# A K/V attention kernel whose V loads are issued from two queues: some of them from ScalarE's, beside transposing K waves on SyncE's

## The chip, the cores and the metric

The kernel runs on one core of one Trainium2 chip. The metric is the device time of a launch in microseconds (us); lower is better. A core has TensorE (matrix multiply, PE in the profile), VectorE (DVE), ScalarE (ACT), GpSimd (POOL) and SyncE (SP), which here issues DMA transfers and nothing else. Each engine runs its own list of instructions in order, and the lists meet in semaphores. All transfers of a core are carried by its 16 DMA engines.

## What is computed

Two attention blocks, A and B, of the same shapes and with inputs of their own. For each of them, with batch 16, 144 query rows, width 448, 16 heads of 256, and 512 cached keys:

```python
q = (x @ wq).reshape(B, Sq, H, Dh).transpose(0, 2, 1, 3)
scores = einsum("bhqd,bhkd->bhqk", q, k_cache) * (Dh ** -0.5)
p = softmax(scores, axis=-1)
o = einsum("bhqk,bhkd->bhqd", p, v_cache)
out = o.transpose(0, 2, 1, 3).reshape(B, Sq, H * Dh) @ wo
```

The results of A and B lie side by side in the last axis of the output. All is bf16. K and V of one (batch, head) pair are 256 KB each; all 512 pairs are read once, K and V, 268 MB in all.

## The kernel before

**Units and steps.** The work is cut into NT = 512 units, one (block, batch, head) each: 0 to 255 are block A ("pass A"), 256 to 511 block B ("pass B"). A main loop over steps `i` writes every engine's list. In step `i` TensorE gets, in this order, the query projection of a unit some steps ahead (`t_q`; mostly for two batches at once), the scores of unit `i` + 3 (`t_s`, line 1112; two steps ahead for the first 48 units), the value product of unit `i` (`t_pv`, line 1168), for every second unit a matmul with ones that adds up the softmax's denominators (line 1184), and a few matmuls of the output projection (line 1284). ScalarE turns scores into exponentials (line 1122, two instructions a unit), and takes logarithm and exponential of the denominators (lines 1192 and 1205), so as to divide. VectorE moves results out of PSUM; GpSimd adds exponentials up. A step takes TensorE some 2 us.

**K.** The scores need K with its head dimension on the partitions. The first 48 units (P0) have K loaded plainly and transposed on TensorE (`t_load_n`, `t_tr`). All later units get theirs by a transposing DMA, in 29 "waves" of 16 units (`t_load_k`, line 988; 4.19 MB each). `kt_sb` holds 32 units (KR), two waves: a wave may be issued once the wave two before it has been used up, so when the scores of its last unit are done.

**V.** A V load (`t_load_v`, line 1002) brings two units (UV), 512 KB. `v_sb` has nine slots (NV), used in turn in the order in which V loads (and the plain K loads of the start) are planned; `ring_free` keeps the step after which each of them is used up, and `v_seq` the place of each load in this order. The slot's semaphore `v0` to `v8` tells TensorE that it has landed.

**Other loads.** `wq` (query weights of a block, in groups of heads), `wo` (output weights, eight groups of 448 KB), and `x` (transposing too, a few batches at a time) are loaded for both blocks; for B as their places come free, which is around the change of pass, near unit 256. Stores of 112 KB go out 36 times.

**Order of the loads.** All DMA is issued from SyncE's queue, in one order that a planner makes at build time. It has a model of TensorE's time (`clock`, read by `at(i)`: when step `i` begins), for each load a due time (`at` of the step of first use, less MARGIN), the step from which its place is free, and a price in us: 1.44 for a V load, 2.0 + 0.97 a unit for a K wave, 1.3 for a wo group, 0.65 a head for wq. It then fills `dma_plan` one by one, keeping `now`, the time at which the DMA engines would be done with what is planned so far, and `slip`, the most that a load has been late. Of the loads that could start first it takes the one that is due first, save that a K wave yields to a load that would be due before the wave were done, and is taken ahead of loads that can wait for it:

```python
elif k_new:
    better = best[1] > start + m[2] + HOLD
```

The main loop then puts each planned load into SyncE's list in the step from which its place is free. SyncE takes them strictly in that order: a load whose place is still in use holds up all that follow.

**Dependencies.** `S.add(engine, ...)` (class `_Sched`) puts an instruction at the end of an engine's list, with waits for all that wrote or read its buffers before, as far as this engine has not waited for it already. So an instruction added to ScalarE's list at the start of step `i` stands ahead of the exponentials of that step, and what it waits for holds up ScalarE.

Of the kernel before, what the change touches and what calls it, by code (L numbers as in the profile page):

```python
# [12 lines left out]
PE, ACT, DVE, POOL, SP = "pe", "act", "dve", "pool", "sp"  # L13
# [110 lines left out]
def _general_path(  # L124
# [48 lines left out]
    NSG = NT // 8  # L173
    NXGT = NP * Bn // XB

# [410 lines left out]
    s_min = -LQ - 24  # L586
    for XG in range(NXGT):
        pr, j = divmod(XG, Bn // XB)
# [164 lines left out]
def bass_concat_heads__mha_block_cached__gqa_block_cached__near_ridge_kernel(  # L753
# [28 lines left out]
    NT = NP * NU  # L782
    UV = 2
# [11 lines left out]
    NV, NX = 9, 6  # L795
# [8 lines left out]
    RC = RS * 128  # L804
    OP_DELAY, OP_START, OP_RATE = 2, (28, 16), (1.04, 1.15)
    MARGIN, HOLD = 1.0, 1.0
    NXGT = len(X_GROUPS)

    P0 = NNAT * UV
# [11 lines left out]
    with contextlib.ExitStack() as es:  # L821
# [35 lines left out]
        S = _Sched()  # L857
# [31 lines left out]
        def of_step(lead, i):  # L889
            return [u for u in (i + lead(0), i + lead(NT)) if 0 <= u < NT and u - lead(u) == i]  # L890
# [100 lines left out]
        def v_source(t, G):  # L991
            pr, b, h0 = unit(UV * G)
            if unit(UV * G + 1)[1] != b:
                return t[pr][b:b + UV, h0].rearrange("u (p c) d -> p u (c d)", p=128)
            return t[pr][b, h0:h0 + UV].rearrange("u (p c) d -> p u (c d)", p=128)

        def t_load_v(G):
            sl = v_seq["v", G] % NV
            src = v_source(vs, G)

            def e(q):
                return q.dma_start(v_sb[:, sl, :, :], src).then_inc(sems["v%d" % sl], 16)  # L1002
            S.add(SP, e, writes=[(("v", sl), ("v", G))], dma_sem="v%d" % sl, name="v%d" % G)

        def t_load_n(G, j=None):
            sl = v_seq["n", G] % NV
# [37 lines left out]
        def q_pair(U):  # L1044

            b, h = unit(U)[1:]
            if U < P0 or h % 2 and b in (0, Bn - 1):
                return 1
            if b % 2 == h % 2:
                return 2  # L1050
            return 0 if U - H >= P0 else 1
# [217 lines left out]
        def chunk_rows(r):  # L1269
            pr, rl = divmod(r, NCH)  # L1270
            row0 = rl * 128
            m = min(128, Bn * SQ - row0)
            return pr, row0, m
# [34 lines left out]
        def t_store(r):  # L1308
            pr, row0, m = chunk_rows(r)
            sl = r % NOST  # L1310

            def e(q):
                return q.dma_start(of[row0:row0 + m, pr * D:(pr + 1) * D], ost_sb[0:m, sl, :]).then_inc(
                    sems["ost%d" % sl], 16)
            S.add(SP, e, reads=[(("ost", sl), r)], dma_sem="ost%d" % sl, name="st%d" % r)
# [62 lines left out]
        def at(i):  # L1378
            return clock[max(i, s_min)]
# [14 lines left out]
        def load_list():  # L1394
            made = []

            def load(use, free, took, fn, *args):
                made.append((at(use) - MARGIN, free, took, fn, args))

            for XG, (g0, g1) in enumerate(X_GROUPS):  # L1400
                load(first_q[g0], (g1 - NX) * H - lq(NT) if g1 > NX else s_min, 1.3 + 0.55 * (g1 - g0), t_load_x, XG)
            for W, (u0, u1) in enumerate(WAVES):
                last = u1 - 1 - KR
                load(u0 - ls(u0), last - ls(last) + 1 if last >= 0 else s_min, 2.0 + 0.97 * (u1 - u0), t_load_k, W)
            for pr in range(NP):
                for h0, h1 in WQ_GROUPS if pr == 0 else [(h, h + 4) for h in range(0, H, 4)]:
                    load(first_h[pr, h0], NU - H + h1 - lq(NU) if pr else s_min, 0.65 * (h1 - h0), t_load_wq, pr, h0, h1)
                for wg in range(NWG):
                    load(wo_use[pr, wg], wo_done[pr - 1, wg] + 1 if pr else s_min, 1.3, t_load_wo, pr, wg)
            for u in range(4):  # L1410
                load(u - LT, s_min, 0.72, t_load_n, u // 2, u % 2)
            for G in range(2, NNAT):
                load(UV * G - LT, None, 1.44, t_load_n, G)
            for G in range(NT // UV):
                load(UV * G, None, 1.44, t_load_v, G)
            return made

        todo = sorted(load_list(), key=lambda m: m[0])
        dma_plan, due, ring_free, now, slip = [], [], [], 2.0, 0.0
        first = [(t_load_n, (0, 0)), (t_load_x, (0,)), (t_load_wq, (0, 0, 1)), (t_load_n, (0, 1))]  # L1420
        v_seq = {("n", 0): 0, ("n", 1): 1}
        ring_free.extend([UV - LT, 2 * UV - LT])
        while todo:
            n = len(ring_free)
            v_lo = ring_free[n - NV] if n >= NV else s_min
            best = None
            for m in todo[:60]:
                lo = v_lo if m[1] is None else m[1]
                start = max(now, at(lo) + slip if lo > s_min else now)
                latest = m[0] + slip - m[2]  # L1430
                if len(first) and m[3:] == first[0]:
                    best = (start, -1e9, m, lo)
                    break
                if best is None or max(start, now) < max(best[0], now):
                    best = (start, latest, m, lo)
                elif max(start, now) == max(best[0], now):
                    k_new, k_old = m[3] is t_load_k, best[2][3] is t_load_k
                    if k_new == k_old:
                        better = latest < best[1]
                    elif k_new:  # L1440
                        better = best[1] > start + m[2] + HOLD
                    else:
                        better = latest <= start + best[2][2] + HOLD
                    if better:
                        best = (start, latest, m, lo)
            if first:
                first.pop(0)
            now, _latest, m, lo = best
            now += m[2] - (1.0 if m[3] is t_load_k and dma_plan and dma_plan[-1][0] is t_load_k else 0.0)
            slip = max(slip, now - m[0])  # L1450
            todo.remove(m)
            dma_plan.append(m[3:])
            due.append(lo)
            if m[1] is None:
                v_seq["n" if m[3] is t_load_n else "v", m[4][0]] = len(ring_free)
                ring_free.append(UV * (m[4][0] + 1) - (LT if m[3] is t_load_n else 0))

        stores = []
        flag_ev = None
        i = s_min  # L1460
        while i < NT or i in op_at or dma_plan or stores:
            while dma_plan and due[0] <= i:
                fn, args = dma_plan.pop(0)
                due.pop(0)
                if fn is t_load_v:
                    while stores and stores[0][1] <= i:
                        t_store(stores.pop(0)[0])
                fn(*args)
            while stores and (stores[0][1] <= i - STORE_LAG or not dma_plan and stores[0][1] <= i):
                t_store(stores.pop(0)[0])  # L1470
            u = i + LT
            if 0 <= u < P0:
                t_tr(u, 0)
            for u in of_step(lq, i):
                if q_pair(u):
                    t_q(u)
                    t_evac_q(u)
            for u in of_step(ls, i):
                t_s(u)
            u = i + LT  # L1480
            if 0 <= u < P0:
                t_tr(u, 1)
            u = i
            if P0 <= u < NT and u % 2:
                t_recip(u)
            if 0 <= u < NT:
                t_pv(u)
                if u < P0 or u % 2 == 0:
                    t_sum(u)
            if u == P0 - 1:  # L1490
                t_pair_ones()
            if P0 <= u + 2 < NT:
                t_halves(u + 2)
            for u in of_step(ls, i):
                t_presum(u)
            u = i
            if 0 <= u < NT:
                if u < P0 or u % 2 == 0:
                    t_ln(u)
                    t_recip(u)  # L1500
                    t_check(u)
                t_evac_ot(u)
                if u == NT - 1:
                    flag_ev = t_flag()
            for bank, r, cs in op_at.get(i, ()):
                t_op_piece(r, cs, bank)
                if cs[-1] == op_last:
                    t_evac_op(r, bank, ACT if bank == "op" else DVE)
                    stores.append((r, i + (2 if i < NT else 0)))
            i += 1  # L1510
# [80 lines left out]
```

## Time and profile before

The time is 1054.97 us (median of three runs, 1054.96 to 1055.44); the profiled execution has a span of 1051.6 us.

| what | before |
|---|---|
| TensorE busy, share of the span | 1029.9 us, 98% |
| ScalarE busy | 794.1 us, 76% |
| VectorE busy | 737.7 us, 70% |
| GpSimd busy | 636.2 us, 61% |
| mean DMA rate | 280 GB/s |
| K waves: count, median from issue to landing | 29, 21.8 us (B) and 21.7 us (A) |
| V loads: count, median from issue to landing | 256, 7.0 us (B) and 6.9 us (A) |

Busy time counts arithmetic alone; issuing a DMA is not counted as busy for the engine that does it, and is shown as the work of its sequencer (SPq for SyncE, ACTq for ScalarE). In a line of the timeline the columns are start and length in us, engine, line of the kernel, operation, output<-input, number of instructions, and in brackets the idle time before it with what ended it. In the table of stretches each row gives a stretch, its length, the busy time of each engine with its number of instructions, and then the granted clock of TensorE, the DMA engines' share (it can be over 1, where packets overlap) and GB/s. The list of waits has total, times and longest, in us.

### The profile page before, as it was taken

The numbers are of one execution on the slowest core, as the hardware profiler recorded it, in microseconds if no ns is written. First come the engines' busy times: TensorE is split into PE (matmuls) and PEld (weight loads), VectorE is DVE, ScalarE is ACT, GpSimd is POOL, SyncE is SP. The second block draws the span as 40 slices with busy tenths as digits, with TensorE's granted clock in tenths as the row PEclk, the third lists the DMA queues.
The fourth block names the chain that finished last, engine by engine and source line by source line (L and its number), as shares of the span: only waits on it lengthen the run. The fifth ranks groups of instructions, "written<-read, shape, count | busy, mean of one in ns | idle before, by whom it ended". The sixth has DMA issues, their size and how long they took to land.

```text
span 1051.6 us, 32329 instructions
## 1 busy us (share of the span) xinstructions
PE 1029.9 (98%) x12376; PEld 875.8 (83%) x12376; DVE 737.7 (70%) x2039; ACT 794.1 (76%) x2365; POOL 636.2 (61%) x1030
## 2 busy tenths in 40 slices
PE   7999999999999999999999799999999999999998
PEld 6999888888888888888888688888888888888885
DVE  5776676777776776676777567677776667777775
ACT  5877677777777787777877567787877777788785
POOL 3555556666666666666756456566666666666673
PEclk9999999999999999999999999999999999999999
DMA  9999999999999999999999999999999999999950
GB/s 291 363 341 340 263 306 266 288 288 293 290 300 284 285 237 257 302 290 297 265 288 340 268 276 300 295 272 300 282 269 269 299 258 305 302 271 257 289 187 14
DMA packets 591748, 294.14 MB, mean 280 GB/s; under 512 B 502592, under 2 KB 516768, under 8 KB 591584
## 3 DMA queue, kind: packets, MB, share of 16 engines
q1 hardware_dynamic: 591584, 291.99, 110.1%
q8 instruction: 99, 1.62, 0.6%
q14 instruction: 65, 0.53, 0.2%
HBM read 161.48 MB, written 4.13 MB: 157 GB/s over the span
## 4 chain that ended last, share of the span: by engine, by line
PE 90%; DMA 6%; SPq 1%; ACT 1%; DVE 1%; issue 0%; POOL 0%; ACTq 0%; DVEq 0%
PE s_ps L1112 23%; PE ot_ps L1168 23%; PE qp_ps L1081 22%; PE op_ps L1284 19%; DMA kt_sb<-in_B_k_cache_dram 2%; DMA kt_sb<-in_A_k_cache_dram 2%; PE ot_ps L1184 2%; DMA wq_sb<-in_A_wq_dram 1%; PE qp_ps L1032 1%; PE s_ps L1032 1%; PE qp_ps L1284 1%; ACT rinv_sb L1205 1%; DMA v_sb<-in_B_v_cache_dram 0%; SPq L1002 0%; ACT pt_sb L1122 0%
## 5 line engine op out<-in xcount | busy, mean ns | idle before, releaser
L1132 POOL TENSOR_TENSOR pp_sb<-pt_sb 128x288 f32<-128x288 bf16 x512 | 384.6, 751 | 320.1 <-ACT pt_sb L1122 305.4
L1122 ACT ACTIVATE pt_sb<-s_ps 128x288 bf16<-128x288 f32 x1024 | 364.6, 408 | 182.7 <-PE s_ps L1112 176.5
L1220 DVE TENSOR_TENSOR ring<-ot_ps,rinv_sb 128x288 bf16<-128x288 f32 (+2 forms) x640 | 241.8, 394 | 159.4 <-ACT rinv_sb L1205 155.0
L1112 PE MATMUL s_ps<-qt_sb,kt_sb 128*128 128x144 bf16 x4096 | 341.3, 227 | 8.0 <-DMA kt_sb<-in_B_k_cache_dram 6.9
L1168 PE MATMUL ot_ps<-pt_sb,v_sb 128*128 128x144 bf16 x4096 | 340.2, 226 | 0.3 <-DMA v_sb<-in_A_v_cache_dram 0.2
L1112 PEld LDWEIGHTS s_ps<-qt_sb,kt_sb 128*128 128x128 bf16 x4096 | 288.3, 98 | 60.0 <-issue 7.3
L1205 ACT ACTIVATE rinv_sb<-ln_sb 64x144 f32<-64x144 f32 x928 | 298.3, 321 | 24.2
L1081 PE MATMUL qp_ps<-xt_sb,wq_sb 128*128 128x288 bf16 (+1 forms) x2368 | 302.3, 271 | 2.2 <-DMA wq_sb<-in_A_wq_dram 1.2
L1284 PE MATMUL op_ps<-wo_sb,ring 128*128 128x448 bf16 x1120 | 285.5, 352 | 0.0
L1081 PEld LDWEIGHTS qp_ps<-xt_sb,wq_sb 128*128 128x128 bf16 x2368 | 212.7, 98 | 77.1 <-DVE qt_sb L1094 2.3
L1168 PEld LDWEIGHTS ot_ps<-pt_sb,v_sb 128*128 128x128 bf16 x4096 | 274.3, 98 | 1.2 <-DMA v_sb<-in_A_v_cache_dram 0.4
L1137 POOL TENSOR_TENSOR p_sb<-pp_sb 128x144 f32<-128x144 f32 x464 | 227.4, 490 | 74.2 <-DVE ps_sb L1146 9.4
L1235 DVE TENSOR_REDUCE run_sb<-ot_ps 128x1 bf16<-128x144 f32 x560 | 146.5, 304 | 76.7 <-ACT ln_sb L1192 42.6
L1146 DVE TENSOR_TENSOR ps_sb<-p_sb 64x144 bf16<-64x144 f32 x464 | 156.1, 336 | 45.8 <-POOL p_sb L1137 32.5
L1095 DVE CAST qt_sb<-qp_ps 128x576 bf16<-128x576 f32 x216 | 162.1, 750 | 14.0 <-PE qp_ps L1081 10.9
L1284 PEld LDWEIGHTS op_ps<-wo_sb,ring 128*128 128x128 bf16 x1120 | 93.7, 98 | 20.1
L1192 ACT ACTIVATE ln_sb<-ot_ps 128x144 f32<-128x144 f32 x232 | 67.9, 293 | 32.3 <-PE ot_ps L1184 24.5
L1184 PE MATMUL ot_ps<-ps_sb,ones 128*128 128x144 bf16 x280 | 63.3, 226 | 0.0
L1094 DVE CAST qt_sb<-qp_ps 128x288 bf16<-128x288 f32 x80 | 35.8, 447 | 2.8 <-PE qp_ps L1081 2.6
L1040 ACT ACTIVATE kt_sb<-qp_ps 128x512 bf16<-128x512 bf16 x48 | 28.9, 603 | 6.1 <-PE qp_ps L1032 6.1
L1137 POOL TENSOR_TENSOR ps_sb<-pp_sb 128x144 bf16<-128x144 f32 x48 | 23.5, 490 | 6.9 <-PE ot_ps L1184 0.3
L1184 PEld LDWEIGHTS ot_ps<-ps_sb,ones 128*128 128x128 bf16 x280 | 27.4, 98 | 0.0
(29 smaller groups left out, 154.5 us busy)
## 6 DMA issues: line engine op xcount, KB each, us to landing
v_sb<-in_A_v_cache_dram SPq DMA_DIRECT2D x128, 512.0 KB, 6.9
v_sb<-in_B_v_cache_dram SPq DMA_DIRECT2D x128, 512.0 KB, 7.0
v_sb<-in_A_k_cache_dram SPq DMA_DIRECT2D x22, 512.0 KB, 9.9
out_dram<-ost_sb SPq DMA_DIRECT2D x36, 112.0 KB, 6.1
wo_sb<-in_A_wo_dram SPq DMA_DIRECT2D x8, 448.0 KB, 8.5
wo_sb<-in_B_wo_dram SPq DMA_DIRECT2D x8, 448.0 KB, 8.7
wq_sb<-in_B_wq_dram SPq DMA_DIRECT2D x4, 768.0 KB, 9.3
wq_sb<-in_A_wq_dram SPq DMA_DIRECT2D x3, 768.0 KB, 9.2
```

What stands on the lines that cost most here:

```text
L1081: ins = t.matmul(acc, lhsT=wq_sb[:, kc, c0:c0 + 128], rhs=xt_sb[:, kc, xo:xe + 1:max(xe - xo, 1), :], start=(kc == 0), stop=(kc == 3))
L1095: return v.tensor_copy(qt_sb[:, a:b + 1:b - a, :, :], qp_ps[:, :, 0:2 * SQ].rearrange("p e (u q) -> p u e q", u=2))
L1112: ins = t.matmul(s_ps[bank][:, (c % 2) * SQ:(c % 2 + 1) * SQ], lhsT=kt_sb[:, 2 * c + dc, ko:ko + 128], rhs=qt_sb[:, qsl, dc, :], start=(dc ...
L1122: return a.activation(pt_sb[:, psl, 2 * k:2 * k + 2, :].rearrange("p b q -> p (b q)"), s_ps[bank][:, 0:2 * SQ], AF.Exp, scale=DH ** -0.5)
L1132: return g.tensor_tensor(pp_sb[:, :, :], pt_sb[:, psl, 0:2, :], pt_sb[:, psl, 2:4, :], op=ALU.add)
L1137: return g.tensor_tensor(dst, pp_sb[:, 0, :], pp_sb[:, 1, :], op=ALU.add)
L1146: return v.tensor_tensor(ps_sb[p0:p0 + 64, sl, :], p2_sb[0:64, :], p2_sb[64:128, :], op=ALU.add)
L1168: ins = t.matmul(ot_ps[ob][:, dc * SQ:(dc + 1) * SQ], lhsT=v_sb[:, vsl, j, c * DH + dc * 128:c * DH + (dc + 1) * 128], rhs=pt_sb[:, sl, c, ...
L1205: return a.activation(rinv_sb[p0:p0 + 64, sl, :], ln_sb[h0:h0 + 64, :], AF.Exp, scale=-1.0)
L1220: ins = v.tensor_tensor(ring[:, 2 * h:2 * h + 2, r0:r0 + q1 - q0], ot_ps[ob][:, 0:2 * SQ].rearrange("p (c q) -> p c q", c=2)[:, :, q0:q1], ...
L1235: return v.tensor_reduce(run_sb[:, k, j:j + 1], ot_ps[ob][:, 2 * SQ:3 * SQ], axis=AX.X, op=op)
L1284: ins = t.matmul(acc[0:m, 0:D], lhsT=ring[:, c, col0:col0 + m], rhs=wo_sb[:, c, :], start=(c == op_first), stop=(c == op_last))
```

## The change

After the planner has placed a K wave that is planned with more than 15 us, it takes up to three of the next V loads out of its list. Each is meant for a moment 3, 7 and 11 us after the wave's start by the model (WITH_K): it is put into the first step at or after that moment in which its slot is free, if that step begins at least 2 us ahead of the end of the wave by the model and the load is due within 40 us of the step; otherwise no more are taken for this wave. `now` grows by 0.9 us for each, where a V load in SyncE's order costs 1.44. At the start of that step the main loop adds the load to ScalarE's list, ahead of the step's exponentials. Slots, semaphores and sources are the same; a V load planned so takes its place in the turn of the slots like any other. The purpose is that V loads need not stand in SyncE's queue behind a wave, and that two queues have packets for the DMA engines while the wave runs.

```diff
--- before.py
+++ after.py
@@ -804,6 +804,7 @@
     RC = RS * 128
     OP_DELAY, OP_START, OP_RATE = 2, (28, 16), (1.04, 1.15)
     MARGIN, HOLD = 1.0, 1.0
+    WITH_K = (3.0, 7.0, 11.0)
     NXGT = len(X_GROUPS)
 
     P0 = NNAT * UV
@@ -994,13 +995,14 @@
                 return t[pr][b:b + UV, h0].rearrange("u (p c) d -> p u (c d)", p=128)
             return t[pr][b, h0:h0 + UV].rearrange("u (p c) d -> p u (c d)", p=128)
 
-        def t_load_v(G):
+        def t_load_v(G, queue=SP):
             sl = v_seq["v", G] % NV
             src = v_source(vs, G)
 
             def e(q):
                 return q.dma_start(v_sb[:, sl, :, :], src).then_inc(sems["v%d" % sl], 16)
-            S.add(SP, e, writes=[(("v", sl), ("v", G))], dma_sem="v%d" % sl, name="v%d" % G)
+            S.add(queue, e, writes=[(("v", sl), ("v", G))], dma_sem="v%d" % sl,
+                  name="%s%d" % ("v" if queue == SP else "va", G))
 
         def t_load_n(G, j=None):
             sl = v_seq["n", G] % NV
@@ -1418,6 +1420,7 @@
         todo = sorted(load_list(), key=lambda m: m[0])
         dma_plan, due, ring_free, now, slip = [], [], [], 2.0, 0.0
         first = [(t_load_n, (0, 0)), (t_load_x, (0,)), (t_load_wq, (0, 0, 1)), (t_load_n, (0, 1))]
+        beside = {}
         v_seq = {("n", 0): 0, ("n", 1): 1}
         ring_free.extend([UV - LT, 2 * UV - LT])
         while todo:
@@ -1454,6 +1457,19 @@
             if m[1] is None:
                 v_seq["n" if m[3] is t_load_n else "v", m[4][0]] = len(ring_free)
                 ring_free.append(UV * (m[4][0] + 1) - (LT if m[3] is t_load_n else 0))
+            if m[3] is t_load_k and m[2] > 15.0:
+                t0 = now - m[2]
+                for dt in WITH_K:
+                    v_lo = ring_free[len(ring_free) - NV]
+                    m = next((m for m in todo if m[3] is t_load_v), None)
+                    step = next(i for i in range(v_lo, NT + 60) if at(i) + slip >= t0 + dt)
+                    if m is None or at(step) + slip > now - 2.0 or m[0] + slip > at(step) + slip + 40.0:
+                        break
+                    todo.remove(m)
+                    beside.setdefault(step, []).append(m[4][0])
+                    v_seq["v", m[4][0]] = len(ring_free)
+                    ring_free.append(UV * (m[4][0] + 1))
+                    now += 0.9
 
         stores = []
         flag_ev = None
@@ -1468,6 +1484,8 @@
                 fn(*args)
             while stores and (stores[0][1] <= i - STORE_LAG or not dma_plan and stores[0][1] <= i):
                 t_store(stores.pop(0)[0])
+            for G in beside.get(i, ()):
+                t_load_v(G, ACT)
             u = i + LT
             if 0 <= u < P0:
                 t_tr(u, 0)
```

## The prediction

> **What bounds the kernel now.** I read the page's busy shares first, then the list of waits, then SyncE's queue in order of time, then the DMA rate in single microseconds.
>
> ```profile
> PE 1029.9 (98%) x12376; PEld 875.8 (83%) x12376; DVE 737.7 (70%) x2039; ACT 794.1 (76%) x2365; POOL 636.2 (61%) x1030
> ...
> q8 instruction: 99, 1.62, 0.6%
> ```
>
> TensorE is busy 1029.9 of 1051.6 us: all that can be won is 21.7 us, and start and tail take about half of that. The list of waits says what is left in the middle:
>
> ```profile
> PE s_ps L1112 <- DMA kt_sb<-in_B_k_cache_dram: 6.9, 1, 6.9
> ...
> PE s_ps L1112 <- DMA kt_sb<-in_A_k_cache_dram: 0.3, 1, 0.3
> ```
>
> One wait of 6.9 us on a K wave, and one of 0.3 us on another. The timeline around each shows which:
>
> ```profile
> 576.58 22.67 SPq L988 DMA_TRANSPOSE kt_sb<-in_B_k_cache_dram  x1
> ...
> 602.01 1.12 PE L1112 MATMUL s_ps<-qt_sb,kt_sb 128*128 128x144 bf16 x8 [6.88 <-DMA kt_sb<-in_B_k_cache_dram]
> ```
> ```profile
> 96.78 17.70 SPq L988 DMA_TRANSPOSE kt_sb<-in_A_k_cache_dram  x1
> ...
> 117.33 0.66 PE L1112 MATMUL s_ps<-qt_sb,kt_sb 128*128 128x144 bf16 x8 [0.34 <-DMA kt_sb<-in_A_k_cache_dram]
> ```
>
> So two of the 29 waves are critical: the wave of units 288 to 303 (issued at 576.58, wanted at 595.1) and the very first, of units 48 to 63. The first misses its moment by only 0.34 us, so anything that delays it goes straight into the time. The other 27 waves land early: comparing each wave's last 256 B packet with the first score matmul that reads it, most have 7 to 14 us to spare; the wave of units 272 to 287 has 4.8.
>
> Now the rate at which the DMA engines work (columns at the end: granted clock, DMA share, GB/s):
>
> ```profile
> 669.00:670.00 1.00, 1.00 (x18) 1.00 (x17) 0.79 (x4) 0.95 (x4) 0.61 (x2) 1.00 0.85 187
> 670.00:671.00 1.00, 1.00 (x11) 0.69 (x9) 0.37 (x2) 0.84 (x3) 0.72 (x1) 1.00 2.71 127
> 671.00:672.00 1.00, 1.00 (x16) 0.93 (x14) 0.85 (x2) 0.22 (x1) 0.50 (x2) 1.00 0.05 6
> 672.00:673.00 1.00, 1.00 (x15) 0.82 (x13) 0.61 (x3) 0.81 (x4) 0.43 (x1) 1.00 1.09 248
> 675.00:676.00 1.00, 1.00 (x14) 0.88 (x12) 0.75 (x2) 0.11 (x2) 0.68 (x2) 1.00 1.28 291
> ...
> 690.00:691.00 1.00, 1.00 (x12) 0.83 (x11) 0.37 (x2) 0.70 (x3) 0.73 (x1) 1.00 1.04 397
> ```
>
> A wave (4.19 MB) moves at 291 GB/s, which would be 14.4 us, but lasts 17 to 20, because it stands still for a while (6 GB/s at 671). The packet records put each of the longer stops beside one 16 KB packet of the instruction queue (q8): while a single DMA engine is held for some 1.0 to 1.3 us, the transposing packets of all 16 stop. V loads move at 397 GB/s: 524,288 B take **1.31 us**. In both kinds of stretch the engines' share is over 1, so they have no idle time except in those stops.
>
> **What the Trainium skill says.** "DMA: Bandwidth & Descriptors", section "Issuing engines are not separate DMA queues": a DMA issued from ScalarE runs on the same 16 engines and interleaves; a second issuer saves only the sequencer's time. The trace can't show a ScalarE issue, but a share over 1 leaves nothing for a second queue to find outside the stops. Same page, "Queues, rings and completion order": each engine takes turns between queues packet by packet. The 16 KB packets inside the waves agree: a foreign packet gets in at once, and the wave waits. "Perfetto Trace Analysis", section "DMA Instruction — HWDGE (DVE, Sync)": the descriptor generator is shared by two sequencers and locked until an instruction's descriptors are made, and that wait is inside the instruction's profiled time. Before, only SyncE issues, so nothing here shows whether ScalarE would share it. "TensorE: Matmul & The Clock Gate", Part 1: after an idle window the array runs at half clock for a few microseconds. The trace agrees: granted clock 0.84 in 600 to 620, and eight projection matmuls took 2.12 instead of 1.14 us.
>
> **The change, part by part.** 28 to 29 waves are long enough (2.0 + 0.97 x 16 = 17.5 planned us, over 15). Beside each, up to three V loads leave SyncE's queue for ScalarE's, in the steps that the planner puts 3, 7 and 11 us after the wave's start. Followed by hand through the planner, all three usually qualify (a V slot comes free each two steps, some 4 us), so some 85 of 256.
>
> ScalarE: 85 issues. A V issue on SyncE takes 0.36 us at least and 0.47 at the median; with packets waiting, 0.5 to 0.6. ScalarE idles about 0.95 us before the exponentials of many steps (waiting for scores), so a cost of 0.5 is hidden by that. The wait that the issue carries (the value matmuls of the slot's last user) belongs to the step before, which TensorE has passed: nothing. Bound above: the lock held for a whole wave, some 14 us. I take 0.5, hence zero.
>
> SyncE: saves 85 x 0.47 us of issue, worth nothing, since it stands waiting for K slots before most waves.
>
> DMA engines: the same bytes. What matters is **c**, the delay of a wave by one V load that cuts in. Lower end near 0 (three V, 3.9 us, all falling into a wave's 3 to 5 us of stops); upper end 2.3 (1.31 plus the 1.0 us or so in which almost nothing moves when a wave gives way to V loads, as at 687). The planner books 0.9 against 1.44 for a V alone. I take **c = 1.4**: the V's own 1.31, a little back from the stops (a V is in flight for a quarter of the wave), a little lost because the 16 engines don't start it at one instant and the wave keeps step with the slowest.
>
> First wave: V 24 to 26 cut in (steps 39, 41, 43, all ahead of step 45 where the wave is wanted). Before, they came after it and were not needed until 124. It lands 3c later with no margin: **+3c = +4.2**.
>
> Waves of pass B: from 497 to 602 the DMA works without a pause, so I add up work. The wave at 497.18 ended at 517.0; 21.7 us of other loads followed, the next wave took 19.5, then 23.7 of V and wo loads, and the critical wave 18.9, to 600.7. After: each of the three waves carries three V (+9c); the gap ahead of the second has four V fewer in front of it by the planner's rule for urgency (the three moved, and V 133, which goes beside it), the gap ahead of the third three fewer: -7 x 1.31 = -9.2. Net 9c - 9.2 = **+3.4**. V 144 and 145, which used to follow the critical wave, now cut into it. The middle wave would land near 561.4 + 1.3 against 562.9, on the edge.
>
> Other waves: 3c = 4.2 later, partly made up by an emptier queue in front of them (their first packets came 1 to 6 us after the slot was free), within margins of 7 to 14: nothing. Wave periods are some 30 us and lateness was made up by about 2.5 us per period after 602, so 3 x (1.4 - 1.31) = 0.3 more per period is carried.
>
> Sum: 12c - 9.2 = 16.8 - 9.2 = **+7.6**, so 1054.97 + 7.6 = **1062.6**. It is zero at c = 0.77, and -9.2 at c = 0.
>
> **Rivals.** (1) The V loads run in the wave's stops, c up to 0.6: the 6.9 us wait and most of its cold matmuls go. For it: 3 to 5 us of stops per wave, and transposing engines that move only 291 of some 400 GB/s. Against: packets of 256 B and 2 KB both show a full share. Time: 12 x 0.2 - 9.2 = -6.8, **1048**. (2) c near 0.77, the gain in pass B pays for the first wave: **1055**. (3) ScalarE's issues take 1 to 2.5 us, as SyncE's did when the queue was full (up to 2.75): about 0.4 us beyond its idle time each, 85 x 0.4 = 34, over 7.6: **1097**. For: the generator may be shared. Against: V issues right behind a wave took 0.58. (4) Locked for the wave: the first V of each waits some 14 us, TensorE runs out after about 3, so 11 x 29 = 320: **1375**. Nothing in the trace speaks for it.
>
> **How the numbers follow.** My forecast (slower by 2 to 20 us) 0.51; (1) 0.20; (2) 0.08; (3) 0.14; (4) 0.07. So faster 0.20, same 0.08, slower 0.72. Low end 1048, the time of (1); high end 1095, which takes c = 2.3 (+18) and most of (3) in, and leaves (4), the worst of (3) and the best of (1) out.
>
> **What would show it.** The wait on the A wave near 117 grows from 0.3 to about 4 us, and the one on the B wave near 602 from 6.9 to about 10; waves last 21 to 24 us from first to last packet; V issues on ScalarE take about 0.5 us; score matmuls wait for ScalarE no more than before. Wrong if waves with V beside them last no longer than now (c small), if the planner orders pass B otherwise than I followed it, or if ScalarE's issues are as long as SyncE's transposes.

## The result and the profile after

The changed kernel takes **1240.81 us** (median of four runs, 1228.79 to 1243.46) against 1054.97: ratio 1.176, with a 95% interval of 1.168 to 1.184. Two further executions took 1246.85 and 1253.39 us. The profiled execution is the shortest of them: a span of 1227.0 us, 175.4 more than before.

The page's first lines, and the queues of its third part (q10 is ScalarE's queue; columns are packets, MB, share of 16 engines):

```profile
PE 1068.8 (87%) x12376; PEld 901.9 (74%) x12376; DVE 738.3 (60%) x2039; ACT 796.5 (65%) x2365; POOL 633.1 (52%) x1030
...
q1 hardware_dynamic: 567920, 246.37, 97.5%
q10 hardware_dynamic: 23664, 45.62, 15.9%
```

The 175.4 us lie on TensorE: it is idle for 158.2 us instead of 21.7 (136.5 more), and its matmuls take 38.9 us longer. No arithmetic was added; the longer matmuls come from the clock (0.938 of full speed granted over the span, 0.996 before): the record has it at half in 20 stretches, 154 us in all where it was 10, and a score matmul takes 320 ns in them instead of 226. What it waits for stands in the list of waits:

```profile
PE s_ps L1114 <- DMA kt_sb<-in_B_k_cache_dram: 70.6, 11, 18.7
PE s_ps L1114 <- DMA kt_sb<-in_A_k_cache_dram: 57.5, 10, 13.7
...
PE qp_ps L1083 <- DMA wq_sb<-in_B_wq_dram: 11.5, 1, 11.5
```

So 21 waves are late, for 128.1 us, where two were late before, for 7.2. The chain that ended last has turned over: 62% DMA and 35% PE, from 6% and 90%.

Next, the issue groups of the waves of pass B, before and after (duration of the issue in ns: least, median, longest):

```profile
L988 SPq DMA_TRANSPOSE kt_sb<-in_B_k_cache_dram x16: 17080/19296/26427, 497.2 to 979.6; - x16
```
```profile
L989 SPq DMA_TRANSPOSE kt_sb<-in_B_k_cache_dram x16: 21950/33278/38351, 572.1 to 1147.8; - x16
```

And the V loads after:

```profile
L1003 SPq DMA_DIRECT2D v_sb<-in_A_v_cache_dram x88: 367/468/2071, 8.5 to 571.5; - x88
...
L1003 ACTq DMA_DIRECT2D v_sb<-in_B_v_cache_dram x47: 374/374/376, 581.6 to 1159.9; - x47
L1003 ACTq DMA_DIRECT2D v_sb<-in_A_v_cache_dram x40: 374/374/434, 100.0 to 577.3; - x40
```

ScalarE's 87 issues take 0.374 us each, nearly without exception: it is not held up. The waves are: the median issue grows from 19.3 to 33.3 us. In the packet records (start, length and queue of every packet) a wave lasts 29.0 us from first to last packet (median of 29), where it lasted 18.0.

One wave in single microseconds (clock, DMA share and GB/s at the end). ScalarE issued its three V loads at 244.06, 247.46 and 251.96; their packets begin at 248.7, 254.3 and 258.7:

```profile
247.00:248.00 1.00, 1.00 (x7) 0.54 (x6) 0.97 (x3) 0.94 (x4) 0.86 (x2) 1.00 1.28 290
248.00:249.00 1.00, 1.00 (x18) 1.00 (x17) 1.00 (x4) 0.73 (x3) 0.61 (x2) 1.00 1.48 316
249.00:250.00 1.00, 1.00 (x10) 0.69 (x8) 0.56 (x3) 0.75 (x3) 0.81 (x1) 1.00 1.01 116
250.00:251.00 1.00, 1.00 (x16) 0.93 (x15) 0.78 (x2) 0.24 (x1) 0.50 (x2) 1.00 1.07 240
251.00:252.00 1.00, 1.00 (x16) 0.82 (x14) 0.62 (x3) 0.81 (x4) 0.46 (x1) 1.00 1.13 226
252.00:253.00 1.00, 1.00 (x17) 0.91 (x15) 0.82 (x3) 0.95 (x4) 0.76 (x2) 1.00 1.36 135
...
264.00:265.00 1.00, 1.00 (x14) 0.82 (x12) 0.79 (x4) 0.95 (x4) 0.59 (x2) 1.00 1.27 284
```

Alone, the wave moves at 290 GB/s. With V packets among its own the two together move at 116 to 240 in the rows shown, and the share of the engines stays above 1: they hold packets and don't move them. In the two half microseconds from 249.0 there are 60 transposing packets and 49 V packets; a wave alone has 1135 in that time, V loads alone some 200. Only at 264, when the third V load is done, has the wave its rate back.

### The profile page after: what moved, and what is told of

Same layout as the page of the kernel before. It is cut to its first block, busy times and chain, and to the rows that moved or that the text cites. A ratio compares the mean times of both kernels' runs of the same rounds, so it can differ in the third digit from the quotient of the medians.

```text
span 1227.0 us, 32329 instructions
## 1 busy us (share of the span) xinstructions
PE 1068.8 (87%) x12376; PEld 901.9 (74%) x12376; DVE 738.3 (60%) x2039; ACT 796.5 (65%) x2365; POOL 633.1 (52%) x1030
## 4 chain that ended last, share of the span: by engine, by line
DMA 62%; PE 35%; SPq 2%; issue 0%; ACT 0%; DVE 0%; ACTq 0%; DVEq 0%
DMA kt_sb<-in_B_k_cache_dram 31%; DMA kt_sb<-in_A_k_cache_dram 29%; PE s_ps L1114 9%; PE ot_ps L1170 8%; PE qp_ps L1083 8%; PE op_ps L1286 7%; DMA wq_sb<-in_A_wq_dram 1%; PE qp_ps L1034 1%; PE ot_ps L1186 1%; PE s_ps L1034 1%; PE qp_ps L1286 0%; SPq L989 0%; DMA wq_sb<-in_B_wq_dram 0%; DMA xt_sb<-in_B_x_dram 0%; SPq L1003 0%
## 5 line engine op out<-in xcount | busy, mean ns | idle before, releaser
L1114 PE MATMUL s_ps<-qt_sb,kt_sb 128*128 128x144 bf16 x4096 | 353.0, 231 | 128.2 <-DMA kt_sb<-in_B_k_cache_dram 70.6
L1114 PEld LDWEIGHTS s_ps<-qt_sb,kt_sb 128*128 128x128 bf16 x4096 | 297.3, 100 | 185.4 <-issue 135.9
L1170 PE MATMUL ot_ps<-pt_sb,v_sb 128*128 128x144 bf16 x4096 | 350.9, 230 | 0.0
L1083 PE MATMUL qp_ps<-xt_sb,wq_sb 128*128 128x288 bf16 (+1 forms) x2368 | 310.3, 276 | 17.5 <-DMA wq_sb<-in_B_wq_dram 11.5
L1286 PE MATMUL op_ps<-wo_sb,ring 128*128 128x448 bf16 x1120 | 293.8, 361 | 0.0
L1083 PEld LDWEIGHTS qp_ps<-xt_sb,wq_sb 128*128 128x128 bf16 x2368 | 216.6, 100 | 99.0 <-issue 17.7
L1170 PEld LDWEIGHTS ot_ps<-pt_sb,v_sb 128*128 128x128 bf16 x4096 | 284.4, 100 | 0.5
## 6 DMA issues: line engine op xcount, KB each, us to landing
v_sb<-in_A_v_cache_dram ACTq DMA_DIRECT2D x40, 512.0 KB, 12.3
```

Source lines behind the costliest of these rows:

```text
L1083: ins = t.matmul(acc, lhsT=wq_sb[:, kc, c0:c0 + 128], rhs=xt_sb[:, kc, xo:xe + 1:max(xe - xo, 1), :], start=(kc == 0), stop=(kc == 3))
L1114: ins = t.matmul(s_ps[bank][:, (c % 2) * SQ:(c % 2 + 1) * SQ], lhsT=kt_sb[:, 2 * c + dc, ko:ko + 128], rhs=qt_sb[:, qsl, dc, :], start=(dc ...
L1170: ins = t.matmul(ot_ps[ob][:, dc * SQ:(dc + 1) * SQ], lhsT=v_sb[:, vsl, j, c * DH + dc * 128:c * DH + (dc + 1) * 128], rhs=pt_sb[:, sl, c, ...
L1286: ins = t.matmul(acc[0:m, 0:D], lhsT=ring[:, c, col0:col0 + m], rhs=wo_sb[:, c, :], start=(c == op_first), stop=(c == op_last))
```

## The experiments

**Theory A**: V packets among transposing packets slow a wave by some 4 us per V load, because the engines can't keep transposing in step. **Rivals**: B, the new order of the loads is at fault; C, a fixed loss as soon as ScalarE's queue is used; D, the loss comes each time V packets start; E, two queues lose rate whatever they carry. Wave lengths below are from first to last packet, from the packet records: a mean over the waves of a run that had all V packets inside as intended, and over all 29 for runs without. The kernel before has 18.0 by this count, the changed one 29.3 (21 waves with three whole V loads inside), so 11.4 more for three. A "start" is a moment at which ScalarE issues V loads. The recorded expectations use earlier counts of the same packets (4.3, 5.3 and 10.7 us for what is 4.5, 5.9 and 11.4 here).

**The changed plan, on SyncE's queue alone.**

```diff
-                t_load_v(G, ACT)
+                t_load_v(G)
```

> The changed plan (same loads taken out, same 0.9 us, same steps), but the loads beside a wave go to SyncE's queue, so that they stand behind the wave. Theory A (V packets among transposing packets slow the wave by about 4 us per V load): no V can mix with a wave, so waves last 17 to 20 us from first to last packet as before and the time is near before, 1045 to 1075 us. Rival B (the new order and its price of 0.9 are at fault, loads reach TensorE too late): time stays near 1240, at least over 1150 us.

Measured: 1064.38 us, ratio 1.0087 (1.0070 to 1.0103). Waves last 17.9 us. Its waits are on V:

```profile
PE ot_ps L1170 <- DMA v_sb<-in_B_v_cache_dram: 9.1, 2, 5.4
...
PE ot_ps L1170 <- DMA v_sb<-in_A_v_cache_dram: 3.6, 1, 3.6
```

B is out as the main cause: the order costs 9 us, since a V load that stands behind a wave comes late; the other 176 us come from the second queue beside the waves.

**One V load beside each wave.**

```diff
-    WITH_K = (3.0, 7.0, 11.0)
+    WITH_K = (3.0,)
```

> One V load beside each wave instead of three (WITH_K = 3.0 alone). Theory A: a wave lengthens by 3.5 to 4.5 us, SyncE's transposing issue from 19 to about 23 us (31 to 33 with three); net of the 1.3 us that the load no longer takes elsewhere and of some 2 us of slack per wave, the time is 1060 to 1095 us. Rival C (a wave loses a fixed time as soon as ScalarE's queue is used at all): waves as long as with three, about 29 us, time over 1180 us.

Measured: 1096.84 us, ratio 1.040 (1.035 to 1.045), at the upper edge of what A gave. In 12 waves the load had run mostly or wholly before the wave's own packets began; these last 18.3 us on the mean. The 17 with at least half of it inside last 22.4, so 4.5 more. C is out: the same queue was used in all of them. The mean hides a spread. Where the load's packets were through in 2.4 to 3.8 us (5 waves), the wave lasted 18.9 to 21.4; where they took 8.5 to 14.0 us (5 waves), 25.0 to 28.3. Inside the longest one:

```profile
232.00:233.00 1.00, 1.00 (x12) 0.74 (x10) 0.76 (x2) 0.95 (x4) 0.47 (x2) 1.00 1.21 64
233.00:234.00 1.00, 1.00 (x13) 0.88 (x12) 0.46 (x2) 0.48 (x2) 0.86 (x2) 1.00 1.33 100
234.00:235.00 1.00, 1.00 (x15) 0.83 (x13) 0.97 (x2) 0.82 (x3) 0.46 (x2) 1.00 1.16 106
```

From 230.0 to 236.5 some nine V packets of 84 ns start per microsecond, about the work of one engine, and the wave gets 290 packets through instead of 1136. That fits one engine after another with V packets left, while the others wait for it; the records don't name a packet's engine, so it isn't shown.

The issue in SyncE's queue is a poorer measure, as it also waits for packets queued ahead:

```profile
L989 SPq DMA_TRANSPOSE kt_sb<-in_B_k_cache_dram x16: 18704/26096/33552, 519.7 to 1028.0; - x16
```

**Three V loads together.**

```diff
-    WITH_K = (3.0, 7.0, 11.0)
+    WITH_K = (11.0, 11.0, 11.0)
```

> Three V loads beside each wave, all at 11 us after its start instead of 3, 7 and 11. Theory A with a cost per V packet: a wave lengthens by about 11 us as with the three apart, time 1200 to 1280 us. Rival D (the cost comes from each start of a V load, when the 16 engines fall out of step): one start instead of three, a wave lengthens by 5 to 7 us, time 1080 to 1150 us.

Measured: 1092.33 us, ratio 1.035 (1.033 to 1.038), with the same 87 V loads on ScalarE's queue. The 25 waves with all three inside last 23.8 us, 5.9 more for three, where three apart cost 11.4. So the cost is not a fixed one per V load, which speaks for D. The microseconds show what a start looks like; V packets begin at 272:

```profile
271.00:272.00 1.00, 1.00 (x15) 0.91 (x13) 0.87 (x3) 0.47 (x2) 0.85 (x2) 1.00 1.28 291
272.00:273.00 1.00, 1.00 (x15) 0.82 (x13) 0.77 (x2) 0.95 (x4) 0.37 (x1) 1.00 1.51 189
273.00:274.00 1.00, 1.00 (x17) 0.93 (x15) 0.46 (x1) 0.95 (x3) 0.86 (x2) 1.00 1.09 70
274.00:275.00 1.00, 1.00 (x9) 0.74 (x8) 0.89 (x5) 0.85 (x3) 0.80 (x2) 1.00 0.84 97
275.00:276.00 1.00, 1.00 (x17) 0.95 (x15) 1.00 (x4) 0.44 (x3) 0.49 (x1) 1.00 1.04 351
276.00:277.00 1.00, 1.00 (x11) 0.63 (x9) 0.54 (x2) 0.95 (x4) 0.57 (x1) 1.00 1.13 397
```

For some 2.3 us next to nothing moves (the median V packet takes 550 to 680 ns instead of 84); then both streams run evenly and together make 351 to 397 GB/s, about what V loads reach alone. **Theory F**, from here on: a V load costs its own 1.31 us, and each start some 2.3 us.

**Plain waves.**

```diff
-                return q.dma_start_transpose(kt_sb[:, :, c0:c0 + n * 128], src).then_inc(sems[sem], 16)
+                return q.dma_start(kt_sb[:, :, c0:c0 + n * 128],
+                                   src.rearrange("(p s) d -> p (s d)", p=128).rearrange("p (c m) -> p c m", c=8)).then_inc(sems[sem], 16)
```

> The changed kernel with K waves loaded by plain copies of the same bytes (descriptors of 4 KB, so K stays untransposed and the scores are of other products). Theory A (the transposing is what can't bear other packets): a wave and its V loads together move at 370 to 410 GB/s, a wave lasts 11 us plus 1.3 for each V, TensorE doesn't wait for K, time 1035 to 1055 us. Rival E (two queues on the same 16 engines lose rate whatever they carry): under 300 GB/s while both are in flight, V loads from ScalarE land after 8 us or more.

Measured: 1044.12 us in its one run, 1055.68 for the kernel before on the same chip. Neither K wave nor V load is waited for. A wave issued at 245.16, with V loads issued at 249.95, 253.75 and 257.93, whose packets begin at 253:

```profile
250.00:255.00 5.00, 5.00 (x61) 4.29 (x59) 3.74 (x11) 3.62 (x12) 3.26 (x6) 1.00 1.03 417
255.00:260.00 5.00, 5.00 (x60) 4.14 (x58) 3.50 (x9) 3.80 (x12) 2.50 (x5) 1.00 1.03 401
```

In the second row both queues are at work, and make 401 GB/s, as much as V loads alone (397): no loss can be seen. E is out. (ScalarE's V loads land after 8.5 and 8.7 us, where V loads took 7.0 and 6.9 before, as they take turns with the wave; so the second half of what E forecast is no sign of a loss.) One thing changed with the transposing: the plain wave has packets of 4 KB instead of 256 B. A plain wave of short packets was not run.

**Two starts.**

```diff
-    WITH_K = (3.0, 7.0, 11.0)
+    WITH_K = (7.0, 11.0, 11.0)
```

> Three V loads beside each wave, one at 7 us and two together at 11 us. Theory F, formed from the first runs: a wave loses 1.3 us per V load plus 2.3 us each time V packets start to run among its packets, since the 16 engines then nearly stop for about that long (one load alone: 4.3 us more; three apart: 10.7; three together: 5.3). So two starts: 3 x 1.3 + 2 x 2.3 = 8.5 us more per wave, a wave from first to last packet about 26.5 us, and a time between those of three together (1092) and three apart (1241), 1140 to 1190 us. Rival A (a cost per V load, the three together cheap for another reason, such as fewer of them inside): as three together, 23 to 24 us, or as three apart, 29 us.

Measured: 1153.65 us, ratio 1.094 (1.090 to 1.098); waves of 26.2 us (27 with three V loads inside), 26.5 forecast. One, two and three starts thus cost 5.9, 8.2 and 11.4 us, where theory F has 3.9 + 2.3 n = 6.2, 8.5, 10.8. Both forms of rival A are out. For one load alone F has 3.6, and 4.5 were measured.

These runs leave a rival that was not tested: with fewer starts the loads also came later. The first V packets run 4.4 us into a wave with three starts, 7.1 with two, 12.3 with one. In the changed kernel itself, 16 waves whose first V packets came in the first 5 us last 30.2 us, the 5 others 26.6. Taking only waves whose first V packets came after 5 us, one, two and three starts give 23.8, 25.8 and 26.6 us (25, 23 and 5 waves). So the number of starts counts, and how early they come seems to count too; the 2.3 us are a mean over both.

**Small loads, on all engines and on one.** Added to the kernel before, with 128 rows in the one run and 127 in the other (`parts` stands for the number here; the tile and its semaphore are left out):

```diff
+        def t_extra(n):
+            src = ks[0].rearrange("b h k d -> (b h k) d")[n * 128:n * 128 + parts, 0:96]
+
+            def e(q):
+                return q.dma_start(extra_sb[0:parts, :], src).then_inc(sems["extra"], 16)
+            S.add(ACT, e, writes=[("extra", n)], dma_sem="extra", name="extra%d" % n)
...
+            if i >= 64 and (i - 64) % 16 in (1, 4) and i < 480:
+                t_extra(i)
```

> The kernel before, with small loads from ScalarE's queue added, two for every 16 steps, at steps where a wave is in flight: 128 rows of 192 B (24.6 KB) into a tile that nothing reads, spread over all 16 engines (8 short packets each). The computation is unchanged. By bytes alone each costs a wave 0.1 us. Theory F: each starts a stop of 1.5 to 2.5 us, so a wave with two of them lasts 21 to 23 us instead of 18, and the time is 1060 to 1110 us. Rival A (only the V load's size matters): waves stay at 18 to 18.5 us, time 1053 to 1060 us.

> As the run before, but 127 rows of 192 B, which all go through one of the 16 engines. The computation is unchanged. If the transposing packets of the 16 engines go forward in step, one engine held for 127 packets (about 2 to 4 us with transposing packets in between) holds all: a wave with two such loads lasts 22 to 27 us, at least as long as with the spread ones, time 1060 to 1150 us. Rival G (engines are independent, only one falls behind by 1/16 of the wave's work): waves of 18 to 20 us, time under 1060 us.

Measured, spread over 16 engines: 1056.72 us, ratio 1.0022 (1.0010 to 1.0033). The packets of one of these loads run from 512.7 to 513.1:

```profile
511.00:512.00 1.00, 1.00 (x12) 0.63 (x9) 0.89 (x3) 0.86 (x4) 0.84 (x2) 1.00 1.28 290
512.00:513.00 1.00, 1.00 (x18) 1.00 (x16) 0.82 (x4) 0.52 (x3) 0.86 (x2) 1.00 1.28 288
513.00:514.00 1.00, 1.00 (x15) 0.82 (x13) 0.65 (x2) 0.98 (x3) 0.33 (x2) 1.00 1.28 289
...
515.00:516.00 1.00, 1.00 (x15) 0.82 (x13) 0.78 (x3) 0.83 (x4) 0.86 (x2) 1.00 0.06 6
```

No stop with the load (the one at 515 follows a 16 KB instruction packet at 514, as in the kernel before), and waves last 18.3 us: theory F as I had put it, a stop for any load that starts, is wrong for these. On one engine, with packets from 531.6:

```profile
531.00:532.00 1.00, 1.00 (x19) 1.00 (x17) 0.82 (x4) 0.52 (x3) 0.81 (x2) 1.00 1.28 290
532.00:533.00 1.00, 1.00 (x15) 0.82 (x13) 0.53 (x2) 0.95 (x4) 0.38 (x1) 1.00 1.30 213
533.00:534.00 1.00, 1.00 (x17) 0.92 (x15) 0.46 (x1) 0.23 (x1) 0.83 (x2) 1.00 1.30 165
```

The same 24 KB, on one engine of 16 (the record has one closing 4 B packet for each of these loads, and sixteen for each of the spread ones), bring the whole wave down from 290 to 165 GB/s for as long as they last (3.3 us). Were the engines independent (G), at most 1/16 of the rate could be lost. About half a microsecond passes first; then 19 small packets and 306 transposing ones, which is 19 for each engine, start in half a microsecond: the wave goes at the pace of the engine that is held. This shows what A took for granted: the transposing packets of the 16 engines go forward in step, with room for some half a microsecond. The run's time (1105.56 us, ratio 1.048) says nothing on this: its second small load waited on ScalarE for the first one, which held the exponentials up for 71.6 us in all. And the wave lengths I had forecast for it (22 to 27 us) did not come: the six waves that held two of these loads in full last 20.8 us, the 26 with any of them 19.6.

**V loads from ScalarE with no wave in flight.**

```diff
-    WITH_K = (3.0, 7.0, 11.0)
+    WITH_K = ()
...
-                fn(*args)
+                fn(*args, *((ACT,) if fn is t_load_v and 6 <= args[0] < 18 else ()))
```

> No V load beside waves; instead twelve V loads of the first 85 us (V 6 to 17), when no K wave is in flight, go from ScalarE's queue, in the same plan as before. Theory F: two queues with plain packets lose nothing, time 1050 to 1060 us, these loads land about as fast as SyncE's. Rival E (ScalarE's queue or its place in ScalarE's list costs something by itself): slower by 5 us or more, TensorE or ScalarE idle in 30 to 85 us.

Measured: 1060.05 us, ratio 1.0063 (1.0007 to 1.0119); these twelve land after 8.5 us (SyncE's own after 6.9 and 7.7), waves last 18.2. It falls on the line between the two forecasts. TensorE's waits on V (0.2 to 1.8 us) and on plain K loads of the start (6.1 to 7.2) grew a little, perhaps as early V loads now run ahead of K loads that are wanted sooner. By itself it settles only that the second queue costs at most 1.2% for twelve loads; for 87 of them the run with plain waves says more.

**V loads of short packets.**

```diff
-                return q.dma_start(v_sb[:, sl, :, :], src).then_inc(sems["v%d" % sl], 16)
+                if queue == SP:
+                    return q.dma_start(v_sb[:, sl, :, :], src).then_inc(sems["v%d" % sl], 16)
+                for c in range(0, 4 * DH, DH):
+                    ins = q.dma_start(v_sb[:, sl, :, c:c + DH], src[:, :, c:c + DH]).then_inc(sems["v%d" % sl], 16)
+                return ins
...
+            S.add(queue, e, writes=[(("v", sl), ("v", G))], dma_sem="v%d" % sl, n_dma=1 if queue == SP else 4,
```

> The changed kernel, but each V load beside a wave is cut along its rows into four transfers of 512 B packets instead of one of 2 KB packets: same bytes, same moments (3, 7, 11 us), 64 short packets on each engine instead of 16 long ones, and four issues on ScalarE (about 1.5 us) instead of one. Theory H (what stops a wave when a V load starts is that a 2 KB packet holds an engine for the time of about six transposing packets, so that the 16 fall out of step; spread short packets of 192 B cost no stop): no start stop, a wave lengthens by 4 to 6 us for the three, 22 to 24.5 us in all, time 1070 to 1130 us, part of it from ScalarE's longer issues. Theory F as it was (any V load that starts costs 2.3 us besides its bytes): 29 us or more (twelve starts), time 1230 us or more.

Measured: 1163.94 us, ratio 1.104 (1.098 to 1.110); waves of 26.6 us (23 with three V loads inside), 8.7 more than before. It lies between the forecasts. Two microseconds of one wave, with V packets in both:

```profile
249.00:250.00 1.00, 1.00 (x8) 0.59 (x6) 0.45 (x1) 0.49 (x2) 0.86 (x2) 1.00 1.33 65
...
251.00:252.00 1.00, 1.00 (x16) 0.88 (x14) 0.88 (x2) 0.77 (x3) 0.14 (x1) 1.00 1.25 269
```

With 512 B packets this wave mostly keeps moving among V packets (136 to 341 transposing packets in each other half microsecond from 246 to 253, where the wave of the changed kernel had some 30 after a start), but stands nearly still at 249 too. The lengthening fell from 11.4 to 8.7 us, so packet length seems to be one cause, and not the only one. The run's time has another part: ScalarE's issues, which here add up to 187 us instead of 33.

## Why the prediction was wrong

**What bounds the kernel; where slack is.** Right as far as it went: the two critical waves, the DMA without a pause in pass B. The first wave now holds TensorE up by 13.7 us at 130.9, as its 3c says with c = 4.6.

**ScalarE's issues cost nothing.** Right: 0.374 us each where 0.5 was taken. Rivals (3) and (4), slower by such issues, rest on a cause that isn't there, and their times, 1097 and 1375, are not near the measured one. The upper end, 1095, took c no higher than 2.3, and counted it in twelve V loads only.

**The step that failed: "I take c = 1.4", with "upper end 2.3".** The runs have 3.7 per V load as changed (29.0 less 18.0, for three), 4.5 for one alone. I had split it into the V load's bytes and a little for engines that don't start together, so the mechanism was named and its size was wrong. The bytes were right (both streams at 397 GB/s once they take turns). What I took for "a little" is the larger part: 2.4 us per V load, in place of 0.1. Not all of it lies at the start: 21 loads that ran alone in a wave of the changed kernel, with no instruction packet near, lose 1.8 us beyond their bytes, 0.7 of it in the first quarter of their packets and 1.1 later. I bounded it by what the trace showed when V follows a wave on one queue, and that is another event: there, no wave goes on behind the V packets. The sign was in the trace before. A single 16 KB instruction packet on one engine stopped all 16, which I read as a stop to be filled; with the run on one engine it reads as engines that transpose in step, so that 48 V packets per engine, if they arrive unevenly, are so many chances to stop all.

**"Other waves: nothing" fell with it.** It rested on 3 x (1.4 - 1.31) = 0.3 us per period against 2.5 of slack. With 3.7 it is 3 x (3.7 - 1.31) = 7.1. From the first wave wanted to the last, 28 periods took 893.05 us before, 31.9 each; now 1052.84, 37.6 each. That is +159.8; the first wave's +13.6 and +2.0 after the last make up the 175.4. The 37.6 are a wave of 29.0, five V loads of 1.31, and 2.0 that remain for x, stores and handing over (a remainder, not measured apart). If as much went there before, a period had 18.0 + 8 x 1.31 + 2.0 = 30.5 us of DMA work in 31.9, an estimated slack of 1.4 where I had 2.5, and 7.1 - 1.4 = 5.7 us more per period are left. This is the measured difference split up, and no second proof of it. Waves used to land 7 to 14 us before they were wanted; that store was gone at the fourth of them. So TensorE, which had waited for 2 waves of 29, waits for 21, and DMA sets the time of most periods.

**Direction and path.** Slower was forecast, through waves made longer by V packets, and so it came. The size was off by a factor of 24 (186 us in the medians, for 7.6).

**Rival (1)**, that V loads run in the wave's stops, is refuted: waves with V loads inside last 4 to 11 us longer. **Rival (2)** needed c near 0.77, a fifth of what was measured.

**What stays open.** That the 16 engines go in step is shown by the run on one engine. Why V packets among transposing ones hold them up, for 2.3 us in one case and over 6 in another, while they share evenly at other times, was not taken apart; V packets left on one engine at a time fit the packet records, and the short packets are only half of an answer. Nor was a start early in a wave set against a late one with all else equal. No run beat the kernel before with K transposed: what the runs say is to keep other packets out of the waves, which it does already.

## What to carry to other kernels

A slack that is shared by many iterations must be checked against the upper bound of the unknown cost, not the value one takes: even c = 2.3 adds 3 x (2.3 - 1.31) = 3.0 us to each period, 1.6 over the slack of 1.4, and 28 periods make 45 us of that, where the prediction had none. Before a second queue is set beside a long transposing transfer, look in the trace for any foreign packet that already lands in one, and see whether one engine or all of them stop. If transfers must share the time of a transposing one, issue them together, once: three in a row, late in the wave, cost half of three apart. Behind the wave they cost less still (1064 us against 1092).

## What the runs showed of the hardware that was not expected

A transposing transfer of 4.19 MB on 16 engines goes at the pace of the slowest one, with some half a microsecond of leeway: 24 KB on one engine bring it from 290 to 165 GB/s. 512 KB loads beside it cost it 2.0 to 2.5 us for each start besides their own bytes, on the mean, in part as near standstill (70 GB/s); a single one lengthened waves to anything from 18.9 to 28.3 us. Plain transfers from both queues share 401 GB/s without loss. An issue from ScalarE during a SyncE issue of over 30 us took 0.374 us, so the two didn't wait for each other; the Trainium skill's "Perfetto Trace Analysis", section "DMA Instruction — HWDGE (DVE, Sync)", describes a descriptor generator that two sequencers share and that is locked for one instruction. No wait for such a lock shows here between SyncE and ScalarE, and the measurement decides.
